# Three queue and order edits in a fused attention and two-MLP kernel: copies from SP's queue, splits three tiles a step, another pace of small work

## The chip, the cores and the metric

The kernel runs on one core of one Trainium2 chip. The metric is device microseconds of the whole program; the number that counts is the median of several runs. A profile is one execution of the same program, and its times are given from the start of its span.

## The reference

Softmax attention with a soft cap, then an MLP with a squared ReLU, then a gated MLP without a nonlinearity, all in float32:

```
scores = cap * tanh(q @ k.T / sqrt(64) / cap)            # 4 batches, 12 heads, 448 x 448
attn   = exp(scores - max) / (sum + 1e-9)
x      = attn @ v                                        # -> [1792, 768]
x      = square(relu(x @ w_in)) @ w_out                  # 768 -> 2048 -> 768
out    = ((x @ w1) * (x @ w2) @ w3) @ w_out2             # 768 -> 1024 -> 1024 -> 768
```

## The kernel before

All matrix products of the MLPs are done in three parts: each operand is split into a high part `h` (rounded to the matmul's format) and a low part `l` (the rest), and TensorE adds `h*h`, `l*h` and `h*l` (`products`, L315 to L320). A split of a tile is one ScalarE (ACT) copy for `h` and one VectorE (DVE) subtraction for `l` (`sub_hi`, L80).

**Attention** is a loop over 84 units `u` (L652 to L708). At a step TensorE (PE) gets the scores of later units (L438, L447), ACT does tanh and exp (L454, L458), DVE adds the exponentials (L468, L474), PE multiplies by v (L487, L494) into PSUM tiles `pv`, which `evacuate` (L516) copies to `acc`. `emit_den` (L503) multiplies the sums by a selector on PE (L513), DVE copies the result to `stg` (L524), and `normalise` takes the reciprocals through DRAM to scale `acc` (L311).

In the same loop the weights of both MLPs are prepared. `w3 @ w_out2` is one matrix that doesn't depend on the data, so it is multiplied out here (L596 to L598) and stored from `cvt` tiles to DRAM (`wp_d`, L610). The first eight half weight tiles of the first MLP ("w0", `w_piece`) are converted in a pool `wq` and copied to DRAM (`w0_d`, named `w_d` in the trace, L580), since the space of `wq` is needed afterwards for the split operands `x0h`, `x0l`, `x1h`, `x1l`. When all of that is done, `w_open` is cleared, `wq` is closed, and eight loads bring the w0 halves back (L687). `splits` (L618) then splits `x0` and `x1`, one tile a step by `advance(side)` (L707), and once `x0` is split `fill` gives PE the first unit of the first MLP: `front` (36 matmuls) and `back` (36 matmuls). An engine works through its instructions in the order in which this program writes them, and so does a DMA queue: an issue that waits holds all issues behind it.

**The first MLP** is a loop over 4 batches and 8 chunks of the hidden dimension; **the second MLP** has two pairs of batches of 8 steps each. A step `s` is `front2` (seven products of 9 matmuls, with combined operands, so that seven do the work of eight) and `back2` (12 groups of 3 matmuls, each added to `acc` by DVE, L842). The PSUM tiles of `back2` have four buffers (`ps_y`). The operands of the second pair are made while the first pair is still computed: `combine2` and `operand` put small pieces of work (one DVE or ACT instruction each) in a list `duties`, and `tick(n)` runs the next n of them: 2 after each product of `front2`, 1 after each group of `back2`. In step 2 there are 16 duties for the sums of the second pair, in step 7 there are 42 for its splits. At step 8, where the pairs change, the halves of `back2(7)` follow directly on the last half of `back2(6)`: 18 groups in a row.

Of the kernel before, what the change touches and what calls it, by code (L numbers as in the profile page):

```python
# [9 lines left out]
F32 = mybir.dt.float32  # L10
# [4 lines left out]
AF = mybir.ActivationFunctionType  # L15
# [6 lines left out]
def tile_kernel(ctx, tc, q, k, v, cap, w_in, w_out, w1, w2, w3t, wo2, out):  # L22
# [21 lines left out]
    PE, ACT, DVE, POOL, SP = nc.tensor, nc.scalar, nc.vector, nc.gpsimd, nc.sync  # L44
# [25 lines left out]
    acc = [stat.tile([128, NP, S], F32, name=f"acc{b}") for b in range(B)]  # L70
# [5 lines left out]
    w0_d = dram.tile([2 * FC, 2, 128, 2, HW], F32, name="w0_d")  # L76
# [65 lines left out]
    def block():  # L142

        return ring.tile([128, 2, HW], F32R, name="wb")
# [121 lines left out]
    def advance(gens, times=1):  # L266
        for _ in range(times):
            for g in list(gens):
                if next(g, "end") == "end":
                    gens.remove(g)  # L270
# [63 lines left out]
    def tick(n):  # L334
        for f in duties[:n]:
            f()
        del duties[:n]
# [51 lines left out]
    with ExitStack() as actx:  # L389
# [8 lines left out]
        NPAIR = B * NP  # L398

        LAST = 3  # L400
        NU = NPAIR // 2 * 7
        loaded, vals, units, pvs, sums, dens = {}, {}, {}, {}, {}, {}
# [21 lines left out]
        def load_v(p):  # L424
            if p < NPAIR:
                b, hp = divmod(p, NP)
                vals[p] = ap_.tile([128, NT, D], F32, name="rv", bufs=3)
                SP.dma_start(out=vals[p], in_=v[b, hp])
# [86 lines left out]

        def evacuate(p):  # L516
            b, hp = divmod(p, NP)
            DVE.tensor_copy(acc[b][:, hp, :], pvs.pop(p))

        def store_den(p):  # L520
            b, g, n = den_group(p)
# [38 lines left out]
        def w_piece(n):  # L560
            kind, i, z = wsrc[n]
            raw = wraw.pop(n)
            if kind == "wo":
                x = block() if i < 5 else wq.tile([128, 2, HW], F32R, name=f"wo{i}{z}")
                parts = [x[:, 0, :], x[:, 1, :]]
            else:
                nj = raw.shape[-1] // 128
                tiles = [wq.tile([128, 3, 128], F32R, name=f"w3{s}", bufs=W3)[:, :nj, :] for s in "hl"]
                parts = [x.rearrange("p a c -> p (a c)") for x in tiles]
            g = narrow(raw, *parts, on=ACT if n >= ON_POOL and n % 2 else DVE, first=POOL if n < ON_POOL else ACT, pool=wq)  # L570
            next(g)
            w_fetch(n + 3)
            for _ in range(LAG):
                yield
            yield from g
            yield
            yield
            if kind == "w0":
                for s, x in enumerate(parts):
                    POOL.dma_start(out=w0_d[i, z, :, s, :], in_=x.bitcast(F32))  # L580
                w3_done.add(wsrc[n])
            else:
                w_ready[wsrc[n]] = parts if kind == "wo" else tiles
# [55 lines left out]
        wnext, chains, side = 0, [], []  # L639
# [5 lines left out]
        for d in range(NPAIR // 2):  # L645
            for x, p in ((7 * d + LAST, 2 * d), (7 * d + 6, 2 * d + 1)):
                later.setdefault((x + 4 | 1) + EVAC, []).append(partial(evacuate, p))
            x = (7 * d + 12 | 1) + 2 * (d == NPAIR // 2 - 1)
# [3 lines left out]
        for u in range(NU + 10):  # L652
            if u < NU and u % 7 in (1, 4):
                load_v(what(u)[0] + 1)
            if 0 <= u - 1 < NU:
                emit_exp(u - 1)
            if u % 2 == 0:
                if u < NU:
                    for x in (u, u + 1):
                        emit_qk(x)  # L660
                    for x in (u, u + 1):
                        emit_tanh(x)
                if w_open:
                    todo = -(-products_left // max((W_END - u) // 2, 1)) if u > W_EVEN else 4
                    for _ in range(todo):
                        x = next(wprod, None)
                        if not x:
                            break
                        products_left -= 1
                    if products_left <= 0:  # L670
                        for _ in wprod:
                            pass
                    if products_left <= 0 and not w_full and not chains:
                        wctx.close()
                        xp = ctx.enter_context(tc.tile_pool(name="x0", bufs=1, side="right", reuse_waits="tile"))
                        for b in range(EARLY):
                            xs[b] = [xp.tile([128, NP, S], F32R, name=f"x{b}{s}") for s in "hl"]
                        new_gtiles(xp)
                        rtiles.extend(cv.tile([128, S], F32, name="cvx", bufs=6) for _ in range(2))
                        w_open = False  # L680
                        fill = first_unit(spare_bank)
                        for _ in range(3):
                            fetch_next()
                        for i in range(2 * FC):
                            halves = [block() for _ in range(2)]
                            for z, x in enumerate(halves):
                                SP.dma_start(out=x.bitcast(F32), in_=w0_d[i, z])  # L687
                            wts[i] = [w for x in halves for w in columns(x)]
                        side.append(splits())
            else:  # L690
                w_store()
                if split_done:
                    next(fill, None)
                for x in (u - 5, u - 4):
                    if 0 <= x < NU:
                        emit_pv(x)
                for f in later.pop(u, ()):
                    f()
            for f in later.pop(u, ()):
                f()  # L700
            if w_open and u > 1 and wnext < len(wsrc) and wnext < min(u, W_FAST) * W_RATE[0] + max(u - W_FAST, 0) * W_RATE[1] and w_may_start(wnext):
                chains.append(w_piece(wnext))
                wnext += 1
            advance(chains)
            if 0 <= u - 4 < NU:
                emit_sum(u - 4)
            advance(side)  # L707
            advance(norms)  # L708
        assert not w_open
        while side:  # L710
            advance(side)
        for _ in fill:
            pass

# [68 lines left out]
    def front2(s):  # L783

        pair = s // NM
        ws = wblk.pop(s)
        ps = [ps_h.tile([128, 512], F32, name="h")[:, :S] for _ in range(7)]
        p1, u2, u3 = (cv.tile([128, S], F32, name="bt", bufs=3) for _ in range(3))
        u4 = spare[1]

        def p(j):
            assert (pair, ORDER[j]) in there
            products(ps[j], ws[j], *place(pair, ORDER[j]))
            if s == NM - 1 and j < 6:
                operand(1, ("B11", "T2", "T3", "B21", "T4", "B22")[j])
            tick(2)

        def add(t, j, u):
            DVE.tensor_tensor(out=t, in0=ps[j], in1=u, op=ALU.add)  # L799

        def gate(j, x, y):
            DVE.tensor_tensor(out=x, in0=x, in1=y, op=ALU.mult)  # L802
            gh, gl = (t[:, s % 2, :] for t in gtiles[j])
            ACT.activation(gh, x, AF.Copy)  # L804
            late.append((gl, x, gh))

        p(0)
        ACT.activation(p1, ps[0], AF.Copy)
        flush()
        p(1)  # L810
        add(u2, 1, p1)
        p(2)
        add(u3, 2, u2)
        p(3)
        add(u4, 3, u3)
        add(u2, 3, u2)
        yield
        p(4)
        add(p1, 4, p1)
        p(5)  # L820
        add(u3, 5, u3)
        gate(0, p1, u3)
        p(6)
        add(u2, 6, u2)
        gate(1, u2, u4)
        yield

    def back2(s):

        pair, m = divmod(s, NM)  # L830
        ws = wpb[s]
        for half in range(2):
            for j, o in product(range(2), range(half * KB, (half + 1) * KB)):
                b = 2 * pair + j
                gh, gl = (t[:, s % 2:s % 2 + 1, :] for t in gtiles[j])
                y = ps_y.tile([128, 512], F32, name="y")[:, :S]
                products(y, [ws[o]], gh, gl)
                a = acc[b][:, o, :]
                if m == 0:
                    ACT.activation(a, y, AF.Copy)  # L840
                else:
                    DVE.tensor_tensor(out=a, in0=y, in1=a, op=ALU.add)  # L842
                if o == half * KB + 1:
                    flush()
                tick(1)
                if m == NM - 1:
                    SP.dma_start(out=out[o * 128:(o + 1) * 128, b * S:(b + 1) * S], in_=a)
            yield
# [36 lines left out]
    for _ in range(2):  # L885
        x = cv.tile([128, 2, HW], F32R, name="bs", bufs=2)
# [79 lines left out]
```

## Time and profile before

| | us |
|---|---|
| runs: median (lowest to highest of 3) | 1063.03 (1062.25 to 1065.13) |
| the profiled execution, its own time | 1064.73 |
| its span, from the first to the last instruction | 1062.8 |
| PE busy in it | 1036.2 |
| DVE busy | 785.3 |
| ACT busy | 535.2 |
| POOL busy | 198.8 |

The first line is the time that a change is measured by. The profiled execution is another one, 1.70 us above that median; 1.93 us of it lie outside the span. PE's busy time counts overlapping matmuls, so a wait of PE shows less in it than in the rate of matmuls.

### The profile page before, as it was taken

What the parts mean: (1) busy time and instruction counts of PE and PEld (TensorE: products, weight loads), DVE (VectorE), ACT (ScalarE), POOL (GpSimd) and SP (SyncE); (2) the same over time, 40 slices, a digit from 0 to 9 for tenths busy, and PEclk for the clock granted to TensorE, in tenths of its full rate; (3) what the DMA queues carried; (4) which work ended last, traced back from release to release, by engine and by line L of the source; (5) the groups of instructions that cost most, each with busy time, mean ns of one, the idle gap of its engine ahead of it and who ended that gap; (6) DMA issues with size and microseconds to landing.
All of it is one profiled execution on the core that took longest, in us unless ns stands there. A gap on an engine that the chain in (4) does not pass through costs nothing.

```text
span 1062.8 us, 14544 instructions
## 1 busy us (share of the span) xinstructions
PE 1036.2 (97%) x5136; PEld 844.9 (79%) x5136; DVE 785.3 (74%) x1485; ACT 535.2 (50%) x946; POOL 198.8 (19%) x360
## 2 busy tenths in 40 slices
PE   7999999997999999999999999999999999999998
PEld 2333555554899999999999999999989997999997
DVE  5999988766576878888788787567386678456666
ACT  7899988873776565555666555441311022300100
POOL 3222223324101011111111101002211322131110
PEclk9999999998999999999999999999999999999999
DMA  6667666663245565655656555126554567566443
GB/s 207 180 176 217 192 191 199 206 212 103 77 117 175 172 174 180 191 182 167 179 178 193 179 166 161 45 57 182 166 177 149 175 211 224 163 206 193 137 149 119
DMA packets 74216, 178.69 MB, mean 168 GB/s; under 512 B 10368, under 2 KB 25760, under 8 KB 74144
## 3 DMA queue, kind: packets, MB, share of 16 engines
q0 software_dynamic: 36992, 97.01, 28.9%
q1 hardware_dynamic: 37008, 80.76, 25.9%
q8 instruction: 40, 0.66, 0.3%
q14 instruction: 32, 0.26, 0.1%
q10 hardware_dynamic: 144, 0.00, 0.0%
HBM read 137.45 MB, written 40.28 MB: 167 GB/s over the span
## 4 chain that ended last, share of the span: by engine, by line
PE 86%; DVE 8%; ACT 3%; DMA 1%; issue 1%; POOL 0%; SPq 0%; DVEq 0%
PE h L320 13%; PE h L318 13%; PE h L319 13%; PE y L318 10%; PE y L319 10%; PE y L320 10%; PE sc L438 3%; PE pv L487 3%; PE h L596 2%; PE h L598 2%; PE h L597 2%; DVE sum L468 1%; ACT pt L458 1%; DVE acc L842 1%; ACT pt L454 1%
## 5 line engine op out<-in xcount | busy, mean ns | idle before, releaser
L319 PE MATMUL y<-gl,wb 128*128 128x448 f32 x372 | 136.4, 367 | 0.0
L320 PE MATMUL y<-gh,wb 128*128 128x448 f32 x372 | 136.3, 367 | 0.0
L318 PE MATMUL y<-gh,wb 128*128 128x448 f32 x372 | 136.3, 366 | 0.0
L799 DVE TENSOR_TENSOR bt<-h,bt 128x448 f32<-128x448 f32 x96 | 59.8, 623 | 91.8 <-PE h L320 75.5
L804 ACT ACTIVATE gh<-bt 128x448 fp32r<-128x448 f32 x32 | 18.5, 578 | 205.0 <-DVE bt L802 205.0
L371 DVE TENSOR_TENSOR acc<-y,acc 128x448 f32<-128x448 f32 x168 | 99.4, 621 | 22.3 <-PE y L320 21.4
L228 POOL DMA_DIRECT2D wc_d<-bs x72 | 38.5, 535 | 333.1 <-DVE cvx L120 158.1
L842 DVE TENSOR_TENSOR acc<-y,acc 128x448 f32<-128x448 f32 x168 | 94.4, 618 | 0.0
L454 ACT ACTIVATE pt<-sc,scl 128x896 f32<-128x896 f32 x84 | 80.5, 1009 | 23.2 <-PE sc L438 17.1
L458 ACT ACTIVATE pt<-pt,capt 128x896 f32<-128x896 f32 x84 | 86.5, 1042 | 0.0
L774 POOL DMA_DIRECT2D wb<-wc_d x112 | 59.4, 544 | 114.2 <-PE h L320 91.0
L438 PE MATMUL sc<-rq,rk 64*128 64x448 f32 x288 | 68.6, 588 | 10.3 <-ACT pt L454 5.3
L318 PEld LDWEIGHTS y<-gh,wb 128*128 128x128 f32 x372 | 69.9, 188 | 6.1
L319 PEld LDWEIGHTS y<-gl,wb 128*128 128x128 f32 x372 | 69.9, 188 | 6.0
L320 PEld LDWEIGHTS y<-gh,wb 128*128 128x128 f32 x372 | 69.9, 188 | 5.9
L318 PE MATMUL y<-gh,raw 128*128 128x448 f32 x192 | 71.6, 373 | 2.4 <-ACT x0h L759 0.8
L80 DVE TENSOR_TENSOR gl<-gr,gh 128x448 fp32r<-128x448 f32 x62 | 38.5, 621 | 47.4 <-ACT gh L354 47.4
L116 ACT ACTIVATE cvx<-raw 128x384 int32<-128x384 uint32 (+1 forms) x136 | 73.4, 540 | 0.0
L113 ACT ACTIVATE cvx<-raw 128x384 f32<-128x384 f32 x124 | 66.8, 539 | 7.3 <-DMA raw<-w_in 3.9
L319 PE MATMUL y<-gl,raw 128*128 128x448 f32 x192 | 70.4, 367 | 0.0
L320 PE MATMUL y<-gh,raw 128*128 128x448 f32 x192 | 70.4, 366 | 0.0
L320 PE MATMUL h<-x2h,wb 128*128 128x448 f32 x192 | 70.2, 366 | 0.0
(166 smaller groups left out, 2527.1 us busy)
## 6 DMA issues: line engine op xcount, KB each, us to landing
wb<-wc_d POOLq DMA_DIRECT2D x112, 384.0 KB, 5.9
wc_d<-bs POOLq DMA_DIRECT2D x72, 384.0 KB, 3.0
raw<-w_in SPq DMA_DIRECT2D x32, 384.0 KB, 3.9
raw<-w_out SPq DMA_DIRECT2D x32, 384.0 KB, 3.9
raw<-w SPq DMA_DIRECT2D x32, 384.0 KB, 3.8
raw<-wc_d POOLq DMA_DIRECT2D x32, 384.0 KB, 3.4
raw<-w3t SPq DMA_DIRECT2D x16, 384.0 KB, 4.2
raw<-wo SPq DMA_DIRECT2D x16, 384.0 KB, 3.3
```

The costliest lines, as they stand in the source:

```text
L113: ACT.activation(a, upper, AF.Copy, scale=2.0 ** -112)
L116: ACT.activation(r, words[:, :, 0], AF.Copy, scale=2.0 ** -29)
L318: PE.matmul(ps, wh, xh[:, i, :], start=start and i == 0, stop=False)
L319: PE.matmul(ps, wh, xl[:, i, :], start=False, stop=False)
L320: PE.matmul(ps, wl, xh[:, i, :], start=False, stop=(i == n - 1))
L371: DVE.tensor_tensor(out=a, in0=y, in1=a, op=ALU.add)
L438: PE.matmul(sc[:, j, :S], rk[r, 128 * t:128 * t + 128], rq[r, :], start=True, stop=True, tile_position=(j * D, 0))
L454: ACT.activation(pt, units[u], AF.Tanh, scale=scl)
L458: ACT.activation(units[u], units[u], AF.Exp, scale=capt)
L774: POOL.dma_start(out=x, in_=wc_d[s % NM, j])
L799: DVE.tensor_tensor(out=t, in0=ps[j], in1=u, op=ALU.add)
L842: DVE.tensor_tensor(out=a, in0=y, in1=a, op=ALU.add)
```

## The change

Four places. The last three `pv` tiles are copied by ACT in place of DVE. The w0 copies are issued from SP's queue, at the same place in the program. `advance(side)` takes three steps at a time from unit 86 on, two after the last. And in the second MLP `tick` runs 3 duties after each product of `front2`, and after a group of `back2` one for odd o and none for even o.

```
         def evacuate(p):
             b, hp = divmod(p, NP)
-            DVE.tensor_copy(acc[b][:, hp, :], pvs.pop(p))
+            a = acc[b][:, hp, :]
+            (ACT.activation(a, pvs.pop(p), AF.Copy) if p >= NPAIR - 3 else DVE.tensor_copy(a, pvs.pop(p)))
...
                 for s, x in enumerate(parts):
-                    POOL.dma_start(out=w0_d[i, z, :, s, :], in_=x.bitcast(F32))
+                    SP.dma_start(out=w0_d[i, z, :, s, :], in_=x.bitcast(F32))
...
                 emit_sum(u - 4)
-            advance(side)
+            advance(side, 3 if u >= NU + 2 else 1)
             advance(norms)
         assert not w_open
         while side:
-            advance(side)
+            advance(side, 3 if u >= NU + 2 else 1)
...
-            tick(2)
+            tick(3)
...
-                tick(1)
+                tick(o % 2)
```

One line is added, so that lines behind L518 have a number one higher in the changed kernel.

PE at the end of attention: `pv` is the last product of attention, `den` the denominators of the last two head pairs, `sc<-x0h` and `sc<-x0l` the 36 matmuls of `front` of the first unit (three of the 36 are shown), `sc<-gh` its `back`.

```order
 L487 MATMUL pv<-pt,rv 64x448 x6
-L513 MATMUL den<-sum,sel 32x448 x4
 L318 MATMUL sc<-x0h,wb 128x448
 L319 MATMUL sc<-x0l,wb 128x448
@@ -538,4 +537,5 @@
 L319 MATMUL sc<-x0l,wb 128x448
 L320 MATMUL sc<-x0h,wb 128x448
+L513 MATMUL den<-sum,sel 32x448 x4
 L318 MATMUL sc<-gh_2441,wb 128x448
```

The four denominator matmuls stood ahead of the first unit and stand between its `front` and its `back` now.

DVE at the same place, before: `sum` is the last head pair's sum of exponentials, `acc_69` the evacuated tiles of the last batch, `x0l` and `x1l` the low parts, `gl` the low part of the first unit's hidden tile.

```order
L524 COPY stg<-den 128x448
L80 TENSOR_TENSOR x0l<-acc_66,x0h 128x448
L468 TENSOR_TENSOR sum<-pt 128x896
L474 TENSOR_TENSOR sum<-sum,pt 64x448 x2
L80 TENSOR_TENSOR x0l<-acc_66,x0h 128x448
L518 COPY acc_69<-pv 128x448
L468 TENSOR_TENSOR sum<-sum,pt 128x896
L80 TENSOR_TENSOR x0l<-acc_66,x0h 128x448 x2
L518 COPY acc_69<-pv 128x448
L80 TENSOR_TENSOR x0l<-acc_66,x0h 128x448 x2
L80 TENSOR_TENSOR x1l<-acc_67,x1h 128x448
```

And DVE there in the changed kernel.

```order
L525 COPY stg<-den 128x448
L80 TENSOR_TENSOR x0l<-acc_66,x0h 128x448
L468 TENSOR_TENSOR sum<-pt 128x896
L474 TENSOR_TENSOR sum<-sum,pt 64x448 x2
L80 TENSOR_TENSOR x0l<-acc_66,x0h 128x448 x3
L468 TENSOR_TENSOR sum<-sum,pt 128x896
L80 TENSOR_TENSOR x0l<-acc_66,x0h 128x448 x2
L80 TENSOR_TENSOR x1l<-acc_67,x1h 128x448 x6
L80 TENSOR_TENSOR gl_2442<-cvx,gh_2441 128x448
L294 SCALAR_TENSOR_TENSOR dt<-dt 128x28
L295 RECIPROCAL dt<-dt 128x28
L80 TENSOR_TENSOR gl_2442<-cvx,gh_2441 128x448
```

The two evacuations left DVE, the second to fourth `x0l` moved ahead of the last sum, and all of `x1l` stands ahead of `gl`.

DVE in steps 7 and 8 of the second MLP, at the end of the 18 groups in a row, before (`acc_66`, `acc_67` are the additions of `back2`, one a group; `x0l` and `x3l` split operands of the second pair).

```order
L842 TENSOR_TENSOR acc_67<-y,acc_67 128x448 x2
L80 TENSOR_TENSOR x0l<-gr_2656,x0h 128x448
L842 TENSOR_TENSOR acc_67<-y,acc_67 128x448
L842 TENSOR_TENSOR acc_66<-y,acc_66 128x448
L80 TENSOR_TENSOR x0l<-gr_2657,x0h 128x448
L842 TENSOR_TENSOR acc_66<-y,acc_66 128x448 x2
L80 TENSOR_TENSOR x0l<-bs,x0h 128x448
L842 TENSOR_TENSOR acc_67<-y,acc_67 128x448 x3
L80 TENSOR_TENSOR x3l<-acc_69,x3h 128x448 x3
```

And the same groups in the changed kernel.

```order
L843 TENSOR_TENSOR acc_67<-y,acc_67 128x448 x3
L843 TENSOR_TENSOR acc_66<-y,acc_66 128x448 x3
L80 TENSOR_TENSOR x0l<-gr_2656,x0h 128x448
L843 TENSOR_TENSOR acc_67<-y,acc_67 128x448 x3
L80 TENSOR_TENSOR x0l<-gr_2657,x0h 128x448
L80 TENSOR_TENSOR x0l<-bs,x0h 128x448
L80 TENSOR_TENSOR x3l<-acc_69,x3h 128x448
```

Two of the three `x0l` splits moved behind the last addition. From the first to the last of the 18 additions DVE had 7 split pieces and 2 `gl` between them; it has 4 and 2 now.

## Rows read from the trace of the kernel before

**Rows 1.** The page: span, and busy time of each engine

```profile
span 1062.8 us, 14544 instructions
...
PE 1036.2 (97%) x5136; PEld 844.9 (79%) x5136; DVE 785.3 (74%) x1485; ACT 535.2 (50%) x946; POOL 198.8 (19%) x360
```

**Rows 2.** Stretches: PE, weight-load, DVE, ACT, POOL busy (instructions), granted clock, DMA share

```profile
247.90:253.30 5.40, 0.89 (x6) 0.09 (x4) 4.94 (x8) 1.04 (x2) 0.57 (x1) 0.92 0.28 77
253.30:259.30 6.00, 5.95 (x16) 4.04 (x17) 4.67 (x10) 0.00 (x0) 0.58 (x2) 0.50 0.01 2
...
778.90:783.80 4.90, 4.21 (x20) 3.23 (x19) 4.87 (x10) 1.16 (x2) 0.00 (x0) 1.00 0.00 0
881.10:895.10 14.00, 12.77 (x56) 9.54 (x55) 13.94 (x27) 5.29 (x11) 2.65 (x5) 1.00 0.63 182
...
940.00:960.00 20.00, 20.00 (x100) 18.43 (x99) 12.79 (x24) 1.70 (x3) 4.76 (x9) 1.00 0.57 177
```

**Rows 3.** The chain that ended last: start us, us, engine, tile

```profile
242.09 0.50 ACT cvt L609
...
242.88 0.53 POOL wp_d L610
243.41 4.79 DMA w_d<-w3h
...
264.60 0.55 ACT cvx L352
...
266.39 0.64 DVE gl L80
```

**Rows 4.** Timeline of POOL: start us, us, instruction [idle before <-releaser]

```profile
238.29 1.03 POOL L303 DMA_DIRECT2D bs<-rec_d  x2 [7.11 <-DVE acc L311]
```

**Rows 5.** Timeline of DVE at the end of attention

```profile
233.01 0.56 DVE L80 TENSOR_TENSOR w3l<-cvt,w3h 128x384 fp32r<-128x384 f32 x1 [1.70 <-ACT w3h L136]
...
244.67 0.62 DVE L524 COPY stg<-den 128x448 f32<-128x448 f32 x1 [1.58 <-PE den L513]
248.31 0.63 DVE L80 TENSOR_TENSOR x0l<-acc,x0h 128x448 fp32r<-128x448 f32 x1 [3.02 <-DMA w_d<-w3h]
...
249.97 1.25 DVE L474 TENSOR_TENSOR sum<-sum,pt 64x448 f32<-64x448 f32 x2
...
252.22 1.07 DVE L468 TENSOR_TENSOR sum<-sum,pt 128x896 f32<-128x896 f32 x1
```

**Rows 6.** Timeline of PE at the end of attention

```profile
245.44 2.48 PE L487 MATMUL pv<-pt,rv 128*64 128x448 f32 x12
...
253.35 1.71 PE L513 MATMUL den<-sum,sel 128*32 128x448 f32 x4 [4.55 <-DVE sum L468]
...
265.99 0.47 PE L319 MATMUL sc<-gl,wb 128*128 128x448 f32 x1 [1.23 <-DVE gl L80]
...
273.75 0.36 PE L318 MATMUL h<-x1h,wb 128*128 128x448 f32 x1
```

**Rows 7.** ACT: timeline, and a group (count, busy us, mean ns, idle before)

```profile
243.41 2.90 ACT L280 ACTIVATE x0h<-acc 128x448 fp32r<-128x448 f32 x6
...
L369 ACT ACTIVATE acc<-y 128x448 f32<-128x448 f32 x18 | 8.9, 540 | 1.9 <-PE y L320 1.9
```

**Rows 8.** SP's queue, timeline; and DMA of 226 to 236 us

```profile
225.29 1.28 SPq L93 DMA_DIRECT2D raw<-w_in  x3
226.66 22.32 SPq L687 DMA_DIRECT2D wb<-w_d  x8
...
DMA packets 1285, 3.37 MB, mean 337 GB/s; under 512 B 159, under 2 KB 293, under 8 KB 1283
```

**Rows 9.** Timeline of DVE in step 2 of the second MLP

```profile
780.35 0.62 DVE L799 TENSOR_TENSOR bt<-h,bt 128x448 f32<-128x448 f32 x1
...
792.60 3.27 DVE L842 TENSOR_TENSOR acc<-y,acc 128x448 f32<-128x448 f32 x6
```

## The prediction, made before the run

> **What bounds the kernel now.** I read the page first. PE is busy for 97% of the span [rows 1], and in the MLPs its matmuls follow each other every 0.202 us (99 weight loads in 20 us at granted clock 1.00, the 2.4 GHz level, in the last of [rows 2]). No edit touches a matmul, so only time that PE loses can be won. I therefore split the span into stretches and looked for those with fewer matmuls or a lower clock. The edits touch two such places.
>
> At the end of attention PE does next to nothing from 247.9 to 253.3, and then runs for 6.0 us at a granted clock of 0.50, the 1.2 GHz level [rows 2]. The chain says why: ACT's store copy, POOL's issue of `wp_d`, a w0 copy that takes 4.79 us to land [rows 3], and only then the first `x0l` on DVE, after 3.02 us of waiting. The last head pair's sum stands behind it on DVE [rows 5], and PE waits 4.55 us for that sum with the denominators, the first unit queued behind them [rows 6]. A smaller wait follows, 1.23 us for `gl` [rows 6].
>
> In the second MLP PE loses time where DVE is late with the additions of `back2` and the four PSUM buffers are full. In the 14.0 us of the 18 groups in a row DVE is busy for 13.94 and PE loads 55 weights, worth 11.1 us [rows 2]: 2.9 us lost. In 4.9 us of step 2 there are 19 where 24 fit, 1.1 us lost, with DVE busy for 4.87 [rows 2].
>
> **The copies.** The last w0 piece is ready when DVE ends `w3l`, at 233.57 [rows 5]. POOL issues its copy only at 243.41 [rows 3]: it sat 7.11 us before 238.29 on a `bs` load that waits for DVE [rows 4], then waited for ACT's copy at 242.09 [rows 3]. On SP nothing of that stands ahead. Its last issues there are three `raw` and eight `wb` loads [rows 8], and the copies are written ahead of those; so they go out at about 233.7, held by their data alone. Landing: 4.79 us as measured, taken twice at worst, gives 238.5 to 243.3. DVE comes to `x0l` at 245.2, when `stg` is through [rows 5]. So the 3.02 us wait goes, and both bounds of the landing leave it at nothing. What it costs: the 11 loads now start behind 233.7 plus two issues, at 234.5, where before they started at 225.3 and 226.7 [rows 8]. That is 11 times 0.393 MB; at the 337 GB/s of ten loaded microseconds [rows 8] the first `front` tile (three raw and two `wb`, 1.97 MB) is in at 240.3 and all of them at 247.3. At 60% of that rate it is 244.2 and 255.9. PE wants the first at 247.9 and the last ones at 257: hidden at both ends. The seven earlier copies stand ahead of loads of q, k, v and weights on SP, two issues each of 0.43 us (three in 1.28, [rows 8]); POOL saves 16 of 0.53 [rows 3]. If each pair held the load behind it back and nothing covered that, 7 times 0.86 makes 6.0 us lost; q, k and v are loaded a head pair ahead of their use and every one of these copies has its data before POOL issues it today, so I take nothing.
>
> The Trainium skill (DMA: Bandwidth & Descriptors, Issuing engines are not separate DMA queues) speaks against this part: DMAs of every issuing engine share the same 16 DMA engines, and another issuer saves only the time to initiate them, usually small. By that rule the move would be worth nothing, POOL not being the bound, and the time is that of the first rival. The trace disagrees in one point: the 9.8 us between ready and issue are queue, not engines.
>
> **DVE and PE there, step by step.** DVE's pieces follow each other every 0.53 us (six in 3.27, [rows 9]); the sum takes 1.07, the two halves 1.25 [rows 5]. From 245.2, in the new order: `x0l` 0 to 245.8; sum and halves to 248.1; `x0l` 1 to 3 until 249.75; last sum to 250.8; `x0l` 4 and 5 to 251.8. PE ends `pv` at 247.92 [rows 6] and goes straight into `front`, as the denominators now stand behind it. A k-step is three matmuls, 0.61 us, so steps 0 to 3 find their `x0l`; step 4 waits 0.65 us. First half done at 252.4, second (18 matmuls, 3.7 us) at 256.1, denominators (0.9: half of 1.71, which ran at clock 0.50 [rows 2, 6]) at 257.0. Then `back` wants `gl`: relu, square and copy on ACT take 1.79 us [rows 3], `gl` 0.64, so with relu 0.2 behind the last matmul the second one is there at 258.7, against a need at 257.8 (fifth matmul): 0.9 us. 36 matmuls later it is 265.3. Before, this point is 273.75 [rows 6]. **Term one: 8.4 us less.** Of it 2.95 us is the half clock, which fell after 4.55 us of idle; the longest gap left is 0.9.
>
> The three evacuations on ACT cost 0.54 each [rows 7], ahead of and among `x0h`, six in 2.90 us [rows 7]. That ends at 247.4, where 250.4 is wanted, and ACT has 1.04 us of work in the 11.4 us behind 247.9 [rows 2]. Without that cover they would cost 1.6. On DVE they free two pieces ahead of `x0l` 5 and one earlier. The last two `x1h` now stand behind the first relu on ACT, `x1l` follows at 256.3 and `gl` at 256.9: just in time, which is why I allow 1 us for it.
>
> **The second MLP.** The total of duties is the same, so this is about where DVE's queue is long. In the 18 groups DVE does 24 pieces from first to last addition in place of 27: 3 times 0.53 is 1.6 us. PE follows DVE only from the sixth group on, so I take two thirds, **1.1 us**; bounds 0 (if groups then wait for `gl` alone) and 2.9 (all that is lost). In step 2 the addition of the last product at 780.35 [rows 9] stands behind two pieces of sums, one of which now comes later, so that the first `back2` addition starts 0.53 us earlier: **0.5 us**, bounds 0 and 1.1. The other way: 3 duties a product put up to 21 pieces, about half of them DVE's, into a `front2` of 12.9 us with 11 pieces of its own; 22 times 0.53 is 11.7, so it fits, but only just; if it didn't, the four PSUM buffers of `front2` cover the first of it. Lower bound 1 us lost.
>
> **The sum.** 8.4 + 1.1 + 0.5 = 10.0 us less. Span 1062.8 [rows 1] becomes 1052.8, the profiled execution 1064.73 becomes 1054.7. That execution is 1.70 above the median of the runs, so as a median **1053.0**. Behind 265.3 PE paces the first MLP; its loads and splits follow PE, so I let the gain stand (the fifth rival is that it doesn't).
>
> **The rivals.**
>
> First: the copies land no earlier in effect, or `x0l` finds another late DMA on the same memory (the `wp_d` store of 242.88 is such a one, on POOL still [rows 3]). Then `x0l` 0 starts at 248.31 as before, and the new order puts `x0l` 5 at 254.9 and the first half's end at 255.4: 3.0 us of term one gone, **1056.0**. For it: 4.79 us for so small a copy; against it: the store fills other tiles than `w3l`, and `x0h` started at 243.41 without waiting [rows 7].
>
> Second: PE's clock falls all the same, since `front` begins in pieces. Six us at 0.50 [rows 2] cost 3.0 us: **1056.0**. Against it: PE is busy from 242 on.
>
> Third: the pace of the second MLP wins nothing, **1054.6**, or loses 1 us, **1055.6**, by the bound above.
>
> Fourth, the other side: SP's head issue holds the 11 loads, and the first weights come late. Each us behind 247.9 then costs one. It eats the whole gain from 257.9 on, that is if 1.97 MB need 23.4 us, 84 GB/s, a quarter of the rate of [rows 8]; at 70 GB/s the kernel is at **1067.7**. Only a copy stuck on SP for another 17 us would do that.
>
> Fifth: term one is won but given back in the first MLP. `x3` is made from denominators that end on PE at 257.0 now, 1.9 us later than before (253.35 and 1.71, [rows 6]), while its use comes 8.4 us earlier; if the way through DRAM in between has less slack than 10.3 us, PE waits for it there, and the second MLP alone is left, **1061.4**. No row here measures that slack; that no wait for `x3` is in the chain says only that there is some.
>
> **How the numbers follow.** Forecast 0.64, its own range 1051.5 to 1055 (the bounds of the second MLP, 1 us for `gl`). First rival 0.11, second 0.10, third 0.06, fourth 0.04, fifth 0.05. No more than 2 in 10 is left out with 1050.0 (all that is lost at both places) to 1057.5. About 0.3%, 3.2 us, is what a measurement of this kernel can tell from no change. All of the first three rivals are faster by more: faster 0.91, same 0.05, slower 0.04.
>
> **What would show it.** w0 copies issued by SP within 1 us of their data, and no wait of `x0l` for a DMA; PE's first matmul on `x0h` at 248 and on `x1h` at 265 to 266; granted clock 1.00 from 242 to 300; four denominators behind the 36th matmul; the 18 groups in 12.5 to 13.2 us. Wrong if SP's `wb` loads land behind 248, if ACT's evacuation waits, or if the weight loads show idle in `front2` of step 2 or 7.

## The result, and the profile after

| | us |
|---|---|
| the changed kernel: median (lowest to highest of 3) | 1054.47 (1054.16 to 1055.21) |
| the kernel before, beside it | 1063.03 (1062.25 to 1065.13) |
| ratio, with its 95% interval | 0.9917 (0.9893 to 0.9940) |
| the profiled execution of the changed kernel, its own time | 1054.16 |
| its span | 1052.2 |

The time fell by 8.56 us as a median, 1.5 less than forecast. Between the two profiled executions it fell by 10.57, and between their spans by 10.6; forecast were 10.0. The page of the changed kernel, its span and the share of each engine (before: [rows 1]):

```profile
span 1052.2 us, 14549 instructions
PE 1031.7 (98%) x5136; PEld 842.9 (80%) x5136; DVE 783.5 (74%) x1482; ACT 536.9 (51%) x949; POOL 190.6 (18%) x344
```

PE has the same matmuls and 4.5 us less busy time. Some 3.0 of it, half of its 6.0 us, is the stretch at half clock, which is gone; 0.84 lies in the 18 groups (12.77 in [rows 2], 11.93 here). The windows show both. They have the columns of [rows 2]: for each engine its busy time and instructions, then the granted clock, the DMA share and GB/s. The first two are the end of attention, the others the second half of step 2 and the 18 groups in a row.

```profile
247.90:253.30 5.40, 4.90 (x24) 3.91 (x23) 5.40 (x10) 2.43 (x5) 0.57 (x1) 1.00 0.33 128
253.30:259.30 6.00, 5.65 (x29) 3.71 (x28) 3.94 (x9) 4.32 (x9) 0.55 (x1) 1.00 0.03 5
770.60:775.00 4.40, 4.21 (x19) 3.24 (x19) 4.37 (x9) 1.16 (x2) 0.00 (x0) 1.00 0.00 0
872.30:885.10 12.80, 11.93 (x55) 9.76 (x55) 12.73 (x25) 4.33 (x9) 2.64 (x5) 1.00 0.58 158
```

The clock stays at its upper level, 2.4 GHz, from attention into the first MLP; before, 253.3 to 259.3 ran at 0.50. SP's queue, where the last w0 copy, the weight loads and the w0 loads stand one behind the other:

```profile
233.82 0.32 SPq L581 DMA_DIRECT2D w_d<-w3l  x1
234.19 1.41 SPq L93 DMA_DIRECT2D raw<-w_in  x3
235.65 6.63 SPq L688 DMA_DIRECT2D wb<-w_d  x8
```

The copy of the last piece leaves at 233.82, when DVE has made it, in place of 243.41 [rows 3]. DVE's timeline there (start, duration, line, tiles, shapes; in brackets the idle time ahead and what ended it):

```profile
244.89 0.62 DVE L525 COPY stg<-den 128x448 f32<-128x448 f32 x1 [2.32 <-PE den L513]
245.43 0.62 DVE L80 TENSOR_TENSOR x0l<-acc,x0h 128x448 fp32r<-128x448 f32 x1
248.26 1.68 DVE L80 TENSOR_TENSOR x0l<-acc,x0h 128x448 fp32r<-128x448 f32 x3
249.86 1.08 DVE L468 TENSOR_TENSOR sum<-sum,pt 128x896 f32<-128x896 f32 x1
250.86 1.15 DVE L80 TENSOR_TENSOR x0l<-acc,x0h 128x448 fp32r<-128x448 f32 x2
258.35 0.62 DVE L80 TENSOR_TENSOR gl<-cvx,gh 128x448 fp32r<-128x448 f32 x1 [0.63 <-ACT gh L354]
```

The first `x0l` follows `stg` without a gap: the 3.02 us of [rows 5] are gone. And PE's timeline:

```profile
245.66 2.48 PE L487 MATMUL pv<-pt,rv 128*64 128x448 f32 x12
248.07 0.47 PE L318 MATMUL sc<-x0h,wb 128*128 128x448 f32 x1
251.53 0.47 PE L319 MATMUL sc<-x0l,wb 128*128 128x448 f32 x1 [0.50 <-DVE x0l L80]
256.44 0.96 PE L513 MATMUL den<-sum,sel 128*32 128x448 f32 x8
258.36 0.47 PE L318 MATMUL sc<-gh,wb 128*128 128x448 f32 x1 [0.16 <-ACT gh L354]
259.02 0.47 PE L319 MATMUL sc<-gl,wb 128*128 128x448 f32 x1 [0.19 <-DVE gl L80]
265.70 0.37 PE L318 MATMUL h<-x1h,wb 128*128 128x448 f32 x1
```

From `pv` PE goes into the first unit, waits once for the fifth `x0l`, and comes to `x1h` at 265.70 instead of 273.75 [rows 6]. The weight loads of the second MLP (first loads of step 2's second half, of what follows it, of the 18 groups and of what follows them, and the longest wait in between):

```profile
770.64 0.19 PEld L318 LDWEIGHTS y<-gh,raw 128*128 128x128 f32 x1
775.02 0.19 PEld L318 LDWEIGHTS h<-x0h,wb 128*128 128x128 f32 x1
872.33 0.19 PEld L318 LDWEIGHTS y<-gh,raw 128*128 128x128 f32 x1
877.29 0.19 PEld L318 LDWEIGHTS y<-gh,raw 128*128 128x128 f32 x1 [1.12 <-ACT x3h L760]
885.13 0.19 PEld L318 LDWEIGHTS h<-x0h,wb 128*128 128x128 f32 x1
```

And the same loads before, without the wait (the 18 groups begin at 881.16 and end at 895.14):

```profile
778.90 0.19 PEld L318 LDWEIGHTS y<-gh,raw 128*128 128x128 f32 x1
783.79 0.19 PEld L318 LDWEIGHTS h<-x0h,wb 128*128 128x128 f32 x1
881.16 0.19 PEld L318 LDWEIGHTS y<-gh,raw 128*128 128x128 f32 x1
895.14 0.19 PEld L318 LDWEIGHTS h<-x0h,wb 128*128 128x128 f32 x1
```

The half of step 2 takes 4.38 us in place of 4.89, the 18 groups 12.80 in place of 13.98. The wait of 1.12 us in the changed kernel belongs to the seventh group and is there before, too, at the same place. The profile puts it down to ACT's `x3h`, but DVE's third addition, from 876.60 to 877.22, ends there as well, and with four PSUM buffers the seventh group wants the buffer that this addition frees.

### The profile page after: what moved, and what is told of

The parts are those of the page before. It is cut to its first block, busy times and chain, and to the rows that moved or that the text cites. A ratio compares the mean times of both kernels' runs of the same rounds, so it can differ in the third digit from the quotient of the medians.

```text
span 1052.2 us, 14549 instructions
## 1 busy us (share of the span) xinstructions
PE 1031.7 (98%) x5136; PEld 842.9 (80%) x5136; DVE 783.5 (74%) x1482; ACT 536.9 (51%) x949; POOL 190.6 (18%) x344
## 4 chain that ended last, share of the span: by engine, by line
PE 87%; DVE 8%; ACT 3%; DMA 1%; issue 1%; SPq 0%; DVEq 0%
PE h L318 14%; PE h L320 14%; PE h L319 14%; PE y L318 11%; PE y L319 11%; PE y L320 11%; PE sc L438 3%; PE pv L487 3%; PE h L597 2%; PE h L599 2%; PE h L598 2%; DVE sum L468 2%; ACT pt L458 1%; DVE sum L474 1%; ACT pt L454 1%; DVE cvt L124 1%
```

## The experiments

Three lengths serve for all of them, since whole traces lie up to 0.9 us apart already where the last `pv` starts: from the last `pv` matmuls to the first on `x1h` (before 273.75 - 245.44 = 28.31 [rows 6], changed 265.70 - 245.66 = 20.04), and those of the 18 groups and of step 2's second half. A second profile of the changed kernel shows how well they repeat:

> The changed kernel once more, as the base for the other three on the same chip: span 1052 to 1053.5, median 1054 to 1055; the 18 groups in 12.8 us, the second half of step 2 in 4.38, x1h 20.0 us behind the start of the last pv matmuls.

20.04, 12.79 and 4.38 us; median 1054.58, ratio 0.9910 (0.9897 to 0.9924).

**The copies back on POOL.**

```
-                    SP.dma_start(out=w0_d[i, z, :, s, :], ...)
+                    POOL.dma_start(out=w0_d[i, z, :, s, :], ...)
```

> The changed kernel with the w0 copies back on POOL, all else as changed. Theory (the copies' place in the queue is what counts): the last copy stands behind the wp_d store again, leaves at 243.4 to 244.0, x0l 0 starts at 248.3 instead of 245.43 and x0l 5 ends at 254.9 instead of 252.0; PE's x1h starts at 268.6 instead of 265.70, the profiled span is 1055.1 instead of 1052.2 and the median 1057.4. If TensorE's granted clock falls in the idle time that this opens, up to 3.0 us come on top (1060.4). Rival (which engine issues a copy makes no difference, since all share the same DMA engines): x1h at 265.7, median 1054.5.

The median is 1056.64, ratio 0.9937 (0.9923 to 0.9950), 2.2 us above the 1054.47 of the changed kernel. In the trace the stretch takes 23.60, 3.56 more. DVE's timeline at the first `x0l`:

```profile
249.01 0.63 DVE L80 TENSOR_TENSOR x0l<-acc,x0h 128x448 fp32r<-128x448 f32 x1 [2.94 <-DMA w_d<-w3h]
```

PE's timeline at the second `x0l`:

```profile
252.52 0.74 PE L319 MATMUL sc<-x0l,wb 128*128 128x448 f32 x1 [1.96 <-DVE x0l L80]
```

And the windows from there on:

```profile
252.50:255.50 3.00, 2.98 (x8) 2.67 (x9) 3.00 (x5) 0.00 (x0) 0.00 (x0) 0.52 0.00 0
255.50:258.50 3.00, 3.00 (x17) 2.73 (x16) 2.25 (x5) 1.46 (x3) 0.00 (x0) 1.00 0.00 0
```

The copy's wait is back, 2.94 us. In this execution the clock fell too, for 3.0 us. The five times are 1055.92 to 1059.86, and the profiled one is the highest: its mean granted clock is 0.997, that of the other four 0.999 or more. Who issues the copy does matter.

**The copies alone**, on the kernel before (the same line, POOL to SP).

> The kernel before with nothing but the w0 copies on SP. Theory: x0l 0 starts at 245.2 to 245.4, the last sum ends at 250.4, PE idles some 2.3 us ahead of the last denominators in place of 4.55; x1h at 267.7 instead of 273.75, clock 1.00, median 1057.0. If the granted clock still falls: up to 3.0 us later, median 1060.0. Rival (which engine issues is worth nothing): x1h at 273.8, median 1063.0.

The stretch takes 22.51: 5.80 less than before. In PE's timeline it still waits for the last sum ahead of the denominators, and for `gl`:

```profile
250.17 0.95 PE L513 MATMUL den<-sum,sel 128*32 128x448 f32 x4 [1.44 <-DVE sum L468]
260.14 0.47 PE L319 MATMUL sc<-gl,wb 128*128 128x448 f32 x1 [1.23 <-DVE gl L80]
267.89 0.37 PE L318 MATMUL h<-x1h,wb 128*128 128x448 f32 x1
```

The clock is 1.00 all through. Median 1058.65, ratio 0.9957 (0.9945 to 0.9970). The rule that the prediction weighed (the Trainium skill, DMA: Bandwidth & Descriptors, Issuing engines are not separate DMA queues) would have this edit worth nothing. With it agrees that the copies land hardly sooner: the medians of the eight copies of each part are 3.3 and 3.6 us here, 3.6 and 3.7 on POOL before. That they run on the same DMA engines no run here shows. What the rule leaves out is the time that an issue stands in its engine's queue behind another one that waits. The last copy landed faster as well, in 2.0 us in the changed kernel against 4.79 before [rows 3], but the earlier issue is enough without that: 233.82 and 4.79 make 238.6, and DVE comes to `x0l` at 245.43. No run left the copies on POOL ahead of the issues that wait, so that it is the place in the queue and not the engine rests on these times.

**The split alone**, on the kernel before.

```
-            advance(side)
+            advance(side, 3 if u >= NU + 2 else 1)
```

> The kernel before with nothing but the split's three tiles a step. Theory: x0l 0 still waits for the copy until 248.3, but PE goes straight into the first unit and the denominators behind it; x0l 4 and 5 come behind an evacuation and the last sum at 254.9 and 255.4; x1h at 269.3 instead of 273.75, median 1058.6, if the clock stays at 1.00; with the fall of before up to 3.0 us later, median 1061.6. Rival (the copy's wait is all there is, the order nothing): x1h at 273.8, median 1063.0.

23.23 us, 5.08 less than before, at clock 1.00, though the copy's wait is there still (2.56 us). PE's timeline has the wait in pieces:

```profile
252.17 0.47 PE L319 MATMUL sc<-x0l,wb 128*128 128x448 f32 x1 [1.94 <-DVE x0l L80]
255.31 0.47 PE L319 MATMUL sc<-x0l,wb 128*128 128x448 f32 x1 [1.02 <-DVE x0l L80]
269.48 0.37 PE L318 MATMUL h<-x1h,wb 128*128 128x448 f32 x1
```

Median of 11 runs 1060.53 (1057.68 to 1063.13), ratio 0.9972 (0.9963 to 0.9981): 3.0 us less than before, not the 5 of the trace, with the widest spread of all kernels here. Part of the difference lies in the two profiled executions. This one is 0.81 us behind already where the last `pv` starts (246.25 against 245.44), as is that of the first experiment (246.22), so that the spans differ by 4.3; and that of before lies 1.2 above the 1063.50 of the executions beside this run. What the other executions lose isn't seen in the profiled one. It has two falls of the clock, but in attention, from 12 to 16 us and from 66 to 71; the window of the second one, in which the clock is 1.00 before:

```profile
60.00:80.00 20.00, 18.50 (x91) 6.67 (x91) 19.07 (x37) 18.47 (x27) 4.39 (x9) 0.91 0.62 188
```

They cost nothing: `pv` matmuls behind them start at 87.32, before at 87.33.

**The changed kernel with the split back at one tile a step.**

> The changed kernel with one tile a step of the split again. The last denominators stand ahead of the first unit on PE once more and wait for the last sum, which DVE now ends at 249.9 (x0l 1 alone ahead of it). Theory: PE idles 1.8 us from 248.1 and 1.8 us for gl; x1h at 267.2 instead of 265.70, span 1053.7, median 1056.0, granted clock 1.00. Rival one (the clock falls in that idle time as it did before the change): up to 3.0 us more, median 1059. Rival two (with the copies early the order makes no difference): x1h at 265.7, median 1054.5.

21.99 us, 1.95 more than the changed kernel; median 1056.80, ratio 0.9939 (0.9927 to 0.9952); clock 1.00. PE waits for the last sum again, but not long:

```profile
250.31 0.95 PE L513 MATMUL den<-sum,sel 128*32 128x448 f32 x4 [0.91 <-DVE sum L468]
```

So in the traces the split is worth 5 us by itself and 2 us once the copies are early, and the copies 5.80 by themselves and 3.56 on top of the split (by the medians 3.0 and 2.3, 4.9 and 2.2): both take away the same idle time. With the copies early the clock stayed up at attention's end in every trace here. With the split alone it did in its own trace, and in that of the first experiment, which has the split and late copies, it fell for 3.0 us.

**The changed kernel with the evacuations on DVE.** This takes back the fourth edit; the title counts the other three.

> The changed kernel with the last three evacuations on DVE again. Theory: one of them comes back between x0l 3 and the last sum, so x0l 4 and 5 are 0.53 us later and the stretch from the last pv matmuls to x1h takes 20.5 to 20.8 us instead of 20.0: 0.5 to 0.8 us slower than the changed kernel. Rival (the evacuations have cover on both engines): 20.0 us, no difference. Rival two (two evacuations ahead of x0l 5 and one ahead of gl, all on PE's path): 21.6 us, 1.6 slower.

20.57, that is 0.53 more, one piece: DVE's sum starts at 250.37 instead of 249.86, and PE's wait at the fifth step shows 1.04 in place of 0.50.

```profile
252.03 0.47 PE L319 MATMUL sc<-x0l,wb 128*128 128x448 f32 x1 [1.04 <-DVE x0l L80]
```

Median 1054.98, ratio 0.9914 (0.9900 to 0.9927), 0.4 above the changed kernel beside it: times alone would not tell this edit from none.

**The changed kernel with the old pace** (`tick(2)`, `tick(1)`).

> The changed kernel with the pace of the small work as it was. Theory: the 18 groups take 13.98 us again instead of 12.80 and the second half of step 2 takes 4.89 instead of 4.38; 1.7 us slower than the changed kernel, all of it at these two places. Rival (DVE's queue is long there for another reason, such as the gates of front2, and the pace moves nothing): the same time as the changed kernel.

13.97 and 4.86; median 1056.21, ratio 0.9924 (0.9912 to 0.9936), 1.6 above the changed kernel beside it. And with one half of that edit, `tick(3)` in `front2` but `tick(1)` in `back2`:

> The changed kernel with three duties behind a product of front2 as changed, but one behind each product of back2 as before. DVE has 27 pieces from the first to the last addition of the 18 groups again, in place of 24. Theory (DVE's pieces among the additions set the pace): the 18 groups take 13.9 to 14.0 us, not 12.80, whatever front2 does. Rival (the win comes from front2, which gets the duties done earlier): 12.8 us.

13.98 us, as the theory said. Unforeseen is step 2, whose half takes 6.52 there by the weight loads:

```profile
771.27 0.19 PEld L318 LDWEIGHTS y<-gh,raw 128*128 128x128 f32 x1
776.17 0.19 PEld L318 LDWEIGHTS y<-gh,raw 128*128 128x128 f32 x1 [2.46 <-DVE acc L843]
777.79 0.33 PEld L318 LDWEIGHTS h<-x0h,wb 128*128 128x128 f32 x1
```

The window behind that has the clock down:

```profile
777.80:784.00 6.20, 6.20 (x24) 5.59 (x23) 3.13 (x6) 0.55 (x1) 3.52 (x7) 0.73 0.66 198
```

Five sums stand among the last additions and gates of `front2` there, and the first addition of `back2` starts at 775.50, 4.2 us behind the first group. This is a single execution, 1059.73.

**A step further.** Five tiles a step, and 4 duties behind each product of `front2`, none in `back2`:

```
-            advance(side, 3 if u >= NU + 2 else 1)
+            advance(side, 5 if u >= NU + 2 else 1)
...
-            tick(3)
+            tick(4)
...
-                tick(o % 2)
+                tick(0)
```

> A further step on the same two theories: five tiles a step at attention's end (x0l 4 and 5 ahead of the last sum, which nothing on PE wants for another 4 us), and four duties behind a product of front2 with none behind one of back2. Theory: PE's wait of 0.65 us at the fifth k-step goes, so x1h comes 0.65 us earlier (19.4 us behind the last pv matmuls); the 18 groups take 11.1 to 11.5 us, PE's own pace, as DVE has 20 pieces of 0.53 us there in place of 24; the second half of step 2 takes 3.7 us. Sum: 2.6 to 3.0 us less than the changed kernel. Rival (28 duties overfill DVE or ACT in front2, with x1h copies ahead of gh on ACT): the wait comes back inside front2 or at its gates, gain 0.65 or less, or a loss of up to 2 us.

The stretch takes 19.29 us, 0.75 less, and PE's wait for `x0l` is gone. The second MLP won nothing: 12.77 and 4.44. DVE's timeline shows why, at the start of the 18 groups:

```profile
872.76 0.63 DVE L80 TENSOR_TENSOR x1l<-acc,x1h 128x448 fp32r<-128x448 f32 x1 [0.58 <-ACT x1h L760]
873.30 0.62 DVE L800 TENSOR_TENSOR bt<-h,bt 128x448 f32<-128x448 f32 x1
873.96 0.63 DVE L803 TENSOR_TENSOR bt<-bt,bs 128x448 f32<-128x448 f32 x1
874.50 1.15 DVE L843 TENSOR_TENSOR acc<-y,acc 128x448 f32<-128x448 f32 x2
876.63 8.96 DVE L843 TENSOR_TENSOR acc<-y,acc 128x448 f32<-128x448 f32 x16
```

No small work stands among the additions any more, but a split piece that waits for ACT stands ahead of the last addition of `front2` (`bt<-h,bt`) and its gate, and so ahead of the first addition of `back2`. Median 1053.69. The next version has the duties ahead of the last two products, 22 in place of 28:

```
-            tick(3)
+            tick((5, 5, 5, 4, 3, 0, 0)[j])
```

> Five tiles a step at attention's end, and the duties placed ahead of front2's last products: 5, 5, 5, 4, 3, 0, 0 behind its seven products and none in back2. In the run with 4 behind each product the pieces behind the sixth and seventh products held up front2's last addition and gate, and so the first addition of back2. Theory: without them the gate ends 0.5 to 1 us earlier, the 18 groups take 11.3 to 11.7 us and the second half of step 2 takes 3.7 to 3.9; with x1h 19.3 us behind the last pv matmuls the sum is 2.3 to 2.8 us less than the changed kernel. Rival (gh and gl of the gates set the start, not the duties): the 18 groups stay at 12.3 to 12.8 and the kernel 0.75 to 1.3 us below the changed one.

DVE's timeline at the same place:

```profile
871.21 0.62 DVE L800 TENSOR_TENSOR bt<-h,bt 128x448 f32<-128x448 f32 x1 [0.57 <-PE h L320]
872.42 1.15 DVE L843 TENSOR_TENSOR acc<-y,acc 128x448 f32<-128x448 f32 x2
```

And the weight loads from the first of the 18 groups to what follows them:

```profile
870.81 0.19 PEld L318 LDWEIGHTS y<-gh,raw 128*128 128x128 f32 x1
875.24 0.19 PEld L318 LDWEIGHTS y<-gh,raw 128*128 128x128 f32 x1 [0.78 <-issue]
882.48 0.19 PEld L318 LDWEIGHTS h<-x0h,wb 128*128 128x128 f32 x1
```

Now DVE waits for PE ahead of that addition, 0.57 us, and not the other way round. The 18 groups take 11.67 with one wait left, and step 2's half 3.67. Span 1049.6, median 1052.10. The kernel before ran 1.8 us faster beside it than beside the 1054.58, so that the two medians can't be compared as they are. Side by side on one chip:

> The changed kernel beside the version with five tiles a step and the early duties, on one chip: 1054 to 1055 if the difference of the traces (2.59 us) is also that of the times.

> The version with five tiles a step and the early duties beside the changed kernel: 2.3 to 2.8 us less than it, by the stretches of the traces (0.75 at attention's end, 1.13 in the 18 groups, 0.71 in step 2). Rival (the chips of the two calls differed, not the kernels): within 1 us of it.

1054.19 and 1051.95: 2.24 us less, ratios to the kernel before 0.9905 (0.9888 to 0.9921) and 0.9884 (0.9869 to 0.9899). This version beats both kernels.

## Why the prediction was right

**Attention's end.** Forecast 8.4 us, measured 8.05 by the start of `x1h` and 8.27 from `pv` on. Step by step, forecast and then measured: the last copy out at 233.7 and 233.82; `x0l` at 245.2 and 245.43; into the first unit at 247.92 and 248.07; denominators from 256.1 and 256.44; the second `gl` through at 258.7 and 259.0; `x1h` at 265.3 and 265.70, of which 0.22 is the later `pv`. The landing of the w0 loads was the one step that came much later. All was to be in at 247.3 (255.9 at the lower rate that was allowed for); the last of the eight, out at about 242, took 9.6 us to land, and the DMA share is still 1.02 from 248 to 249, 0.59 in the next microsecond and 0.06 in the one after. The prediction had named `wb` loads landing behind 248 as a sign of being wrong. It came, and the sum held all the same, since PE wanted the last ones only at 257 and waited for none.

**Its parts.** 2.95 us were put down to the half clock. No run takes the clock alone away. Where the long wait of 4.55 us was broken up, the windows of this stretch show 1.00, except for the 3.0 us of the first experiment. The price of a copy that comes late, 3.0 in the first rival, is 3.56 in that trace and 2.2 by the medians. Some 0.6 of the 3.56 goes to the clock: the matmul on the fifth `x0l` starts 1.29 us behind the start of its split there (255.75 and 254.46), 0.67 in the changed kernel (251.53 and 250.86), and 2.94 of wait and 0.62 make 3.56. This is argued from the times, not shown by a run. The evacuations were put at two pieces on DVE; one, 0.53 us, is on the path.

**The second MLP.** Forecast 1.1 and 0.5, measured 1.18 and 0.51. The mechanism is DVE's pieces among the additions: 27 in the 18 groups make 13.97 or 13.98 us, with two as with three duties a product of `front2`; 24 make 12.80, 20 make 11.67 if nothing holds up the first. The factor of two thirds came out by some luck. Its reason was that PE follows DVE only from the sixth group on; but the first ten groups run alike in both traces (the tenth starts 7.14 us behind the first one before, 7.13 now). The gain arises behind them, where DVE has the three pieces less, and there PE runs the last six groups at its own pace of 0.61 us each, so that the last one starts 1.29 us earlier and not 1.6. Leaving the longer `front2` at nothing was right only with both halves of the edit: with `tick(3)` alone step 2 loses 2.14 us and more behind it.

**The rivals.** The first, second and third fell as shown, the first one closely: in the chain of the changed kernel what released the first `x0l` last is one of the w0 loads, now behind the copies in SP's queue:

```profile
237.31 8.14 DMA wb<-w_d
```

It lands just as `stg` is through. In all ten profiles with early copies `x0l` starts 0.54 or 0.55 us behind the start of `stg`, one piece, so it cost nothing; but a load that lands later would show. The fourth: SP's eight loads are all out at 242.28, and PE's only waits up to 270 are the three above. The fifth: from `x1h` to step 2's second half it is 770.64 - 265.70 = 504.94 us, before 778.90 - 273.75 = 505.15 ([rows 6], and the start of the window in [rows 2]), and no wait of PE in that trace names the `x3` of the first MLP, so it is waited for nowhere.

**The sum.** 8.27 less 0.22 for the later `pv`, 0.21 in the first MLP, 0.51, 0.06, 1.18 and 0.09 behind make 10.10, the difference of PE's last matmuls (1057.56 before, 1047.46 after). The other 0.5 of the span lies behind PE, in the landing of the last store. What was off is a small term, the way from the profiled execution to the median, which the prediction took as unchanged: the one before lay 1.70 above its median, the one after 0.31 below. These 2.01, less the 0.54 by which the profiled time came out lower than forecast, are the 1.47 between 1053.0 and 1054.47. The runs show what the 1.70 goes with. In the 38 executions of the kernel before beside the experiments, 21 had a mean granted clock of 0.997 or more and a median of 1062.95, 17 had less and a median of 1064.51; the profiled one had 0.996. The 11 of the changed kernel all had 0.998 or more. So the 1.70 goes with lost clock, of which the change takes the most away; that the clock is its cause is likely, not shown. The kernel before has medians from 1062.59 to 1064.39 here, the changed kernel 1054.19 to 1054.58. The difference of 8.56 in the first three runs is thus a low one; the other two times that both were run side by side it was 9.81 and 9.99.

## What to carry to other kernels

An issue that has its data and stands in a queue behind one that has not goes out late by what the other one waits (9.8 us here); what that costs is what waits for its landing (3.02 us on DVE, and what PE waited behind that). Move it to a queue whose head is not late there, and look at what then stands behind it. Where an engine's small work is spread over a loop, look for the instruction that hands over to the next stage (here the last addition and gate of `front2`): pieces ahead of it cost their full time there, and nothing where the engine is idle. Two edits that remove the same idle time don't add, so price each one with the other in place.

## What the runs showed of the hardware

The clock need not take a wait of 4.55 us to fall. A wait of 1.96 us (with 0.60 shortly ahead of it) was followed by 3.0 us at 0.52, and one of 2.46 us in the middle of the second MLP by 6.2 us at 0.73 on average; waits of 1.94 and 1.02, of 1.44 and of 0.91 us were followed by 1.00. So of two waits as long as 1.94 and 1.96 one cost clock and the other didn't. In attention a wait of 1.50 us ahead of 64.97 was followed by 0.50 from 68 to 70 us with the split alone, and one of 1.49 us at the same place of the kernel before by 1.00. These runs don't tell what decides it. Nor does a fall always cost time: the one in attention cost none, so PE was not what bounded that stretch. A stretch without such a fall repeats to some hundredths of a microsecond (20.04 and 20.04, 12.80 and 12.79, 4.38 and 4.38), while the intervals of the ratios here are 2 to 5 us wide: a cost of 0.5 us is read from two traces, not from medians.
